# One core, banded attention and two MLPs: a planned order for all engines, and gate and value in seven block products out of eight

## The chip, the core and the metric

The kernel runs on one core of a Trainium2 chip. TensorE (PE in the profile) multiplies; its stationary operand is loaded by separate instructions (PEld). VectorE (DVE), ScalarE (ACT) and GpSimd (POOL) work on elements, and SyncE (SP) issues the transfers. Each engine runs its instructions in the order of the program and waits on semaphores for the others. The metric is device time in microseconds of one execution; less is better. The median of three runs of the kernel before is 694.55 us (694.54 to 695.88).

## What is computed

Sixteen attentions of 768 tokens (two batches, eight heads of 64), where a query sees itself and the 95 keys before it, and the first 8 keys of its sequence; then an MLP with a squared relu, a normalisation, and a gated MLP. All is float32 to the reference's accuracy.

```python
scores = scale * q @ k.T + bias;  scores = where(is_global | is_local, scores, -1e9)
a = softmax(scores);  x = (a @ v)                     # 1536 tokens x 512
h = maximum(x @ w_in, 0);        x = (h * h) @ w_out  # 512 -> 2048 -> 512
xn = x / sqrt(mean(x * x) + 1e-6) * rms_g
g = xn @ w_gate;  x = (g * sigmoid(g) * (xn @ w_val)) @ w_out2   # 512 -> 1536 -> 512
```

## The kernel before

Every product of the MLPs is taken in three: each operand is kept as a rounded high part and a low part (float32r), and `mm3` adds high by high, high by low and low by high (L158 to L160). A product has a stationary block of 128x128 and 512 moving columns. The tokens are handled in three chunks `c` of 512.

**Weights** come as float64 blocks of 128x512 (68 of them). `Weights.split` turns one into its two float32r parts: an absolute value on ACT (L103), four steps on DVE (L104 to L110), a rounding copy on ACT (L112) and a subtraction on DVE (L113). Eight slots, then sixteen, hold them.

**Attention** goes by 48 tiles of 128 queries and two heads. `qk` (L453) makes six score products of up to 256 columns, two heads side by side in the array; DVE adds the bias and takes the extreme (L458); ACT takes the exponential (L462); `scale` inverts the sums (L471, L472) and POOL multiplies by them (L474); `transpose` (L484) turns the blocks on TensorE and ACT copies them out (L486); `pv` (L499) multiplies by the values, and once a chunk and head pair is full, ACT and DVE split the result (L506, L507). POOL also rounds the keys and queries (L431) and builds the biases (L536, L541).

**The first MLP** (`stage1`) runs over 4 groups `g` of hidden blocks and the chunks: four hidden blocks (`ph`, 48 products), relu and square split into two parts, and four output blocks (`py`, 48 products) added to `y`. **The normalisation** (`queue_norm`) is a list of small steps that `tick` hands out between products; it has one product with a matrix of ones (`pn`, L276). **The second MLP** (`stage2`) runs over 4 groups and 3 chunks: for three blocks a gate product (`pg`) and a value product (`pv`, L160), Silu on ACT (L313), the multiplication on DVE (L320), the split, and the output product (`po`), added to `o` by DVE (L196).

**The order** is that of the program's text, which the tile framework's scheduler may then move. The text runs the attention as events; from event 60 on, each event gives the MLP a credit of 0.45 products of three (`RATE`, `MLP_FROM`). The 13 products of `warm_up` keep TensorE at work before the first scores.

Of the kernel before, what the change touches and what calls it, by code (L numbers as in the profile page):

```python
# [2 lines left out]

# [21 lines left out]
CH = 512  # L25
# [31 lines left out]
class Weights:  # L57
# [6 lines left out]
    LEAST = 2.0**-15  # L64
    MOST = float(np.array([0x47EFFFFF], np.int32).view(np.float32)[0])

    def __init__(self, nc, pool, srcs, slots):
        self.nc, self.pool, self.srcs = nc, pool, srcs
        self.stage, self.hl, self.slot = {}, {}, {}
        self.nload = self.nsplit = self.freed = 0  # L70
        self.idle = deque()
        self.nslots = 0
        self.add_slots(pool, slots)

    def add_slots(self, pool, slots):
        for _ in range(slots):
            self.idle.append((pool, self.nslots))
            self.nslots += 1

    def load(self):  # L80
        n = self.nload
        if n >= len(self.srcs):
            return
        t = self.pool.tile([P, 512, 2], I32, tag="wraw", bufs=2, name=f"wraw{n}")
        src = self.srcs[n].bitcast(I32)
        self.nc.sync.dma_start(out=t.rearrange("p c w -> p (c w)"), in_=src)
        self.stage[n] = t
        self.nload += 1

    def split(self):  # L90
        n = self.nsplit
        if n >= len(self.srcs) or not self.idle:
            return False
        while self.nload <= n:
            self.load()
        nc = self.nc
        raw = self.stage.pop(n)
        pool, s = self.slot[n] = self.idle.popleft()
        t = self.pool.tile([P, 512], I32, tag="wbits", bufs=2, name=f"wbits{n}")
        hi = pool.tile([P, 512], F32R, tag=f"whi{s}", bufs=1, name=f"whi{n}")  # L100
        lo = pool.tile([P, 512], F32R, tag=f"wlo{s}", bufs=1, name=f"wlo{n}")
        low, high = raw[:, :, 0], raw[:, :, 1]
        nc.scalar.activation(f32(t), f32(high), AF.Abs)  # L103
        nc.vector.tensor_scalar(  # L104
            out=f32(t), in0=f32(t), scalar1=self.LEAST, scalar2=self.MOST, op0=ALU.max, op1=ALU.min)
        nc.vector.tensor_scalar(
            out=t, in0=t, scalar1=3, scalar2=0x3FFFFFF8, op0=ALU.logical_shift_left, op1=ALU.bitwise_and)
        nc.vector.scalar_tensor_tensor(  # L108
            out=t, in0=low, scalar=29, in1=t, op0=ALU.logical_shift_right, op1=ALU.bitwise_or)
        nc.vector.scalar_tensor_tensor(  # L110
            out=t, in0=high, scalar=-(1 << 30), in1=t, op0=ALU.bitwise_and, op1=ALU.bitwise_or)
        nc.scalar.copy(hi, f32(t))  # L112
        nc.vector.tensor_tensor(out=lo, in0=f32(t), in1=f32(hi), op=ALU.subtract)  # L113
        self.hl[n] = (hi, lo)
        self.nsplit += 1
        self.load()
        return True

    def get(self, n):
        while self.nsplit <= n:  # L120
            assert self.split(), (n, self.freed)
        return self.hl[n]

    def free(self, n):
        for i in range(self.freed, n):
            self.hl.pop(i)
            self.idle.append(self.slot.pop(i))
        self.freed = max(self.freed, n)


class Mlp:
    def __init__(self, nc, main, late, psum, weights, gcol, epst, ones, out):
        self.nc, self.main, self.late, self.psum = nc, main, late, [psum]
        self.banks = {psum: MB}
        self.w, self.gcol, self.epst, self.ones, self.out = weights, gcol, epst, ones, out
        self.x = {}
        self.xk = {}
        self.z = {}
        self.y = {}
        self.bg = deque()  # L140
        self.zdone = set()
        self.tick_n = 0

    def new_act(self, c, name):
        hi = self.main.tile([P, KD, CH], F32R, tag="acth", bufs=NC_, name=f"{name}h{c}")
        lo = self.main.tile([P, KD, CH], F32R, tag="actl", bufs=NC_, name=f"{name}l{c}")
        return hi, lo
# [22 lines left out]
    def ready(self, c, k):  # L170
        return self.xk.get(c, 0) > k
# [693 lines left out]
```

## Time and profile before

| | us |
|---|---|
| median of three runs | 694.55 |
| the profiled execution, from the first to the last instruction (span) | 694.5 |
| TensorE busy | 676.2 (97%) |
| VectorE, ScalarE, GpSimd busy | 434.0, 298.3, 85.8 |
| last attention product ends, about | 164 |
| last product of all begins | 686.4 |

The profiled execution's time and its span agree with the median of the runs, so that sums are made against 694.5. An engine's busy time counts instructions in flight; products of TensorE overlap, and so 97% busy doesn't say that it works at its peak. What a product costs is read from the distance between the starts of two that follow each other. The granted clock is 1.00 for 2.4 GHz and 0.50 for 1.2 GHz.

### The profile page before, as it was taken

How to read it: one execution, taken by the hardware profiler on the slowest of the kernel's cores; microseconds unless marked ns; L12 is line 12 of the kernel's file. 1: busy time of each engine (PE TensorE's matmuls, PEld its weight loads, DVE VectorE, ACT ScalarE, POOL GpSimd, SP SyncE). 2: the span in 40 equal slices, each digit the busy share in tenths (PEclk: the TensorE clock that was granted, in tenths of full speed). 3: DMA queues.
4: the chain of work that ended last, by engine and by line, in shares of the span. 5: the costliest groups of instructions: out<-in, count | busy, mean ns of one | idle time of the engine just before them, and what ended most of it. 6: DMA issues, size and time to landing. Idle time of an engine off the chain costs nothing.

```text
span 694.5 us, 9041 instructions
## 1 busy us (share of the span) xinstructions
PE 676.2 (97%) x3283; PEld 538.4 (78%) x3283; DVE 434.0 (62%) x949; ACT 298.3 (43%) x625; POOL 85.8 (12%) x154
## 2 busy tenths in 40 slices
PE   6999999999999999999999999999999999999995
PEld 4666676676888888888888888888888888888884
DVE  6678936656889598448878995386239833322232
ACT  4555955866764254224456563443114411211110
POOL 6654724541000000000000000000000000000000
PEclk8568999999999999999999999999999999999998
DMA  7334523111334133004400221044003200001011
GB/s 245 125 129 158 187 72 105 60 63 56 128 121 135 49 100 112 30 1 122 121 1 20 73 91 61 4 147 122 0 1 114 98 1 0 1 1 60 1 60 67
DMA packets 16421, 52.84 MB, mean 76 GB/s; under 512 B 2416, under 2 KB 2928, under 8 KB 16368
## 3 DMA queue, kind: packets, MB, share of 16 engines
q1 hardware_dynamic: 16368, 52.18, 22.8%
q8 instruction: 28, 0.46, 0.3%
q14 instruction: 25, 0.20, 0.1%
HBM read 49.03 MB, written 3.15 MB: 75 GB/s over the span
## 4 chain that ended last, share of the span: by engine, by line
PE 75%; DVE 0%; ACT 0%; issue 0%; DVEq 0%
PE py L158 6%; PE py L160 6%; PE py L159 6%; PE ph L158 5%; PE ph L160 5%; PE ph L159 5%; PE pg L159 5%; PE pv L159 5%; PE pg L158 5%; PE pv L158 5%; PE pg L160 5%; PE pv L160 5%; PE po L158 5%; PE po L159 5%; PE po L160 5%; PE pn L276 0%
## 5 line engine op out<-in xcount | busy, mean ns | idle before, releaser
L159 PE MATMUL ph<-xl,whi 128*128 128x512 f32 x192 | 77.1, 402 | 0.0
L158 PE MATMUL ph<-xh,whi 128*128 128x512 f32 x192 | 75.5, 405 | 1.4 <-ACT xh L506 1.1
L160 PE MATMUL ph<-xh,wlo 128*128 128x512 f32 x192 | 75.6, 395 | 0.0
L103 ACT ACTIVATE wbits<-wraw 128x512 f32<-128x512 f32 x68 | 45.7, 673 | 69.5 <-DMA wraw<-in_w_out_dram 19.5
L320 DVE TENSOR_TENSOR s<-pv,sg 128x512 f32<-128x512 f32 x36 | 24.8, 689 | 70.3 <-PE pv L160 70.2
L112 ACT CAST whi<-wbits 128x512 fp32r<-128x512 f32 x68 | 41.9, 617 | 57.7 <-PE ph L159 22.8
L474 POOL TENSOR_SCALAR p<-p,rs 128x256 f32<-128x256 f32 (+1 forms) x96 | 55.9, 594 | 55.7 <-DVE rs L472 30.4
L113 DVE TENSOR_TENSOR wlo<-wbits,whi 128x512 fp32r<-128x512 f32 x68 | 46.4, 684 | 19.8 <-ACT whi L112 19.6
L462 ACT ACTIVATE p<-p,mn 128x256 f32<-128x256 f32 (+1 forms) x96 | 46.7, 488 | 23.8 <-DVE mn L458 22.6
L158 PE MATMUL pg<-zh,whi 128*128 128x512 f32 x144 | 56.4, 392 | 0.0
L160 PE MATMUL pg<-zh,wlo 128*128 128x512 f32 x144 | 56.0, 389 | 0.0
L159 PE MATMUL pg<-zl,whi 128*128 128x512 f32 x144 | 56.0, 389 | 0.0
L159 PE MATMUL pv<-zl,whi 128*128 128x512 f32 x144 | 56.0, 389 | 0.0
L160 PE MATMUL pv<-zh,wlo 128*128 128x512 f32 x144 | 56.0, 389 | 0.0
L158 PE MATMUL pv<-zh,whi 128*128 128x512 f32 x144 | 56.0, 389 | 0.0
L458 DVE CUSTOM_DVE_ANT_0 p<-ps,bw 128x256 f32<-128x256 f32 x80 | 32.5, 419 | 33.0 <-PE ps L453 27.6
L313 ACT ACTIVATE sg<-pg 128x512 f32<-128x512 f32 x36 | 21.5, 596 | 70.9 <-PE pg L160 70.6
L110 DVE SCALAR_TENSOR_TENSOR wbits<-wraw,wbits 128x512 int32<-128x512 int32 x68 | 47.2, 694 | 0.7
L108 DVE SCALAR_TENSOR_TENSOR wbits<-wraw,wbits 128x512 int32<-128x512 int32 x68 | 47.1, 693 | 0.2
L196 DVE TENSOR_TENSOR o<-po,o 128x512 f32<-128x512 f32 x36 | 22.7, 685 | 37.3 <-PE po L160 37.3
L158 PEld LDWEIGHTS ph<-xh,whi 128*128 128x128 f32 x192 | 36.2, 191 | 9.8 <-ACT xh L506 1.6
L159 PEld LDWEIGHTS ph<-xl,whi 128*128 128x128 f32 x192 | 36.4, 190 | 9.2 <-issue 2.1
(130 smaller groups left out, 1477.9 us busy)
## 6 DMA issues: line engine op xcount, KB each, us to landing
wraw<-in_w_out_dram SPq DMA_DIRECT2D x28, 512.0 KB, 3.4
wraw<-in_w_in_dram SPq DMA_DIRECT2D x16, 512.0 KB, 3.5
wraw<-in_w_gate_dram SPq DMA_DIRECT2D x12, 512.0 KB, 3.5
wraw<-in_w_val_dram SPq DMA_DIRECT2D x12, 512.0 KB, 3.5
v<-in_vab_dram SPq DMA_DIRECT2D x8, 512.0 KB, 3.6
out_dram<-o SPq DMA_DIRECT2D x12, 256.0 KB, 2.2
raw<-in_kq_dram SPq DMA_DIRECT2D x4, 624.0 KB, 3.8
raw<-in_kq_dram SPq DMA_DIRECT2D x4, 608.0 KB, 3.6
```

The source lines that it names most:

```text
L103: nc.scalar.activation(f32(t), f32(high), AF.Abs)
L108: nc.vector.scalar_tensor_tensor(out=t, in0=low, scalar=29, in1=t, op0=ALU.logical_shift_right, op1=ALU.bitwise_or)
L110: nc.vector.scalar_tensor_tensor(out=t, in0=high, scalar=-(1 << 30), in1=t, op0=ALU.bitwise_and, op1=ALU.bitwise_or)
L112: nc.scalar.copy(hi, f32(t))
L113: nc.vector.tensor_tensor(out=lo, in0=f32(t), in1=f32(hi), op=ALU.subtract)
L158: nc.tensor.matmul(ps, lhsT=w[0], rhs=a[0], start=first, stop=False)
L159: nc.tensor.matmul(ps, lhsT=w[0], rhs=a[1], start=False, stop=False)
L160: nc.tensor.matmul(ps, lhsT=w[1], rhs=a[0], start=False, stop=last)
L320: nc.vector.tensor_tensor(out=s, in0=pv, in1=sg, op=ALU.mult)
L458: nc.vector.tensor_tensor_reduce(out=p[:, j, :w], in0=ps[j][:, :w], in1=bias, scale=-0.125, scalar=3.0e38, op0=ALU.add, op1=ALU.min, accum ...
L462: nc.scalar.activation(p[:, j, :w], p[:, j, :w], AF.Exp, bias=mn[:, j : j + 1], scale=-1.0, accum_out=sm[:, j : j + 1])
L474: nc.gpsimd.tensor_scalar(out=p[:, j, :w], in0=p[:, j, :w], scalar1=rs[:, j : j + 1], scalar2=1.0, op0=ALU.mult, op1=ALU.mult)
```

## The change

1. **A plan sets the order on every engine.** All work is first recorded as operations (`Plan.add`) with an engine, an estimated duration, what they read and write, and a due time. `solve` runs a list scheduling over the estimates, and `emit` writes the operations in the order of their planned starts. The framework's own scheduler is off for this part (`manual_schedule`). Attention tiles have due times from `FIRST`, `PACE0` and `PACE1`.
2. **Chunks of 384 tokens**, four instead of three. The two products of the first MLP now have 384 moving columns. The output product of the second keeps 512.
3. **The first MLP begins earlier and is spread.** As soon as the attention of a chunk is complete, the 96 products of group 0 for that chunk stand between the attention steps of the next chunk (chunks 0 to 2).
4. **Gate and value by the Strassen-Winograd scheme.** Two weight blocks and two chunks form a 2x2 block product, done in seven products (`PRODUCTS`) instead of eight. Sums of weight blocks are made by POOL and split (`pair`), sums of activations likewise (`norm`); partial results are joined in PSUM by copies on ACT and additions on DVE (`quad`).
5. **Low parts on POOL.** Most of the subtractions that make the low part of a weight move from DVE to POOL, which has no such operation before.
6. **Squares on ACT.** `relu2` is three ACT operations and one on DVE for all groups.
7. **Fillers.** 76 products of a zeroed tile stand in gaps of the plan up to its 30th microsecond, in place of the 13 of `warm_up`.

```diff
-CH = 512
+CH = 384
+FIRST, STEP, PACE0, PACE1 = 8.0, 2.0, 2.1, 2.9
+FILL = 30.0
...
+class Plan:
...
+    def solve(self):
+        for o in reversed(self.ops):
+            for q in o.succ:
+                o.due = min(o.due, q.due - o.dur - (o.lat if q.eng != o.eng else 0.0))
...
+            t, e = best
+            while wait[e] and wait[e][0][0] <= t:
+                o = heappop(wait[e])[2]
+                heappush(ready[e], (o.due, o.n, o))
+            o = heappop(ready[e])[2]
...
+            if e == "PE" and t < FILL and filling:
+                x = max(free[e], 1.0)
+                while x + 0.2 < t:
+                    self.fill.append(x)
+                    x += 0.18
...
+    def emit(self, filler=None):
+        todo = [(o.start, 1, o.n, o.emit) for o in self.ops]
+        if filler:
+            todo += [(x, 0, i, filler) for i, x in enumerate(self.fill)]
+        for x in sorted(todo, key=lambda x: x[:3]):
+            x[3]()
...
+PRODUCTS = {
+    1: ("A11", "B11"), 2: ("A12", "B21"), 3: ("S4", "B22"), 4: ("A22", "T4"),
+    5: ("S1", "T1"), 6: ("S2", "T2"), 7: ("S3", "T3")}
...
+    def split(self, src, dst, n, rs, ws, eng):
+        e, t = (nc.vector, DVE) if eng == "DVE" else (nc.gpsimd, POOL2)
+        self.op("ACT", ACT(n), lambda: nc.scalar.copy(dst()[0], src()), rs, [(x, "hi") for x in ws])
+        self.op(eng, t(n), lambda: e.tensor_tensor(
+            out=dst()[1], in0=src(), in1=f32(dst()[0]), op=ALU.subtract), rs + [(x, "hi") for x in ws], [(x, "lo") for x in ws])
...
+    def pair(self, key, slots):
+        a, ra = self.expand()
...
+        self.split(a, sl.get, 512, ra, sl.res, "POOL")
+        keep(("A11", "A12"), sl)
+        b, rb = self.expand()
...
+        add(R(s, 0), R(b, 0), R(b, 1), ALU.add, rb, rs)
+        add(R(s, 1), R(s, 0), R(a, 0), ALU.subtract, rs + ra, rs)
+        sl2 = slots()
+        self.split(s, sl2.get, 512, rs, sl2.res, "POOL")
+        keep(("S1", "S2"), sl2)
+        sl3 = self.half_slot()
+        self.split(R(b, 1), lambda: tuple(two(t) for t in sl3.get()), 256, rb, sl3.res, "DVE")
+        keep(("A22",), sl3, 1)
+        add(R(b, 0), R(a, 0), R(b, 0), ALU.subtract, ra + rb, rb)
+        add(R(b, 1), R(a, 1), R(s, 1), ALU.subtract, ra + rs + rb, rb)
+        sl4 = slots()
+        self.split(b, sl4.get, 512, rb, sl4.res, "POOL")
+        keep(("S3", "S4"), sl4)
...
+    def quad(self, key, p, banks, sink):
+        self.product(1, b1, key, p, True)
+        self.op("ACT", ACT(CH), lambda: nc.scalar.copy(ps[b2](), ps[b1]()), rb(b1), rb(b2))
+        self.product(5, b3, key, p, True)
+        self.op("ACT", ACT(CH), lambda: nc.scalar.copy(p5(), ps[b3]()), rb(b3), r5)
+        self.product(6, b2, key, p, False)
+        self.op("DVE", DVE(CH), lambda: nc.vector.tensor_tensor(
+            out=ps[b3](), in0=ps[b2](), in1=p5(), op=ALU.add), rb(b2) + r5, rb(b3))
+        self.product(2, b1, key, p, False)
+        sink(0, 0, ps[b1], rb(b1))
+        self.product(7, b2, key, p, False)
+        self.op("DVE", DVE(CH), lambda: nc.vector.tensor_tensor(
+            out=t(), in0=ps[b2](), in1=p5(), op=ALU.add), rb(b2) + r5, rt)
+        sink(1, 1, t, rt)
+        self.product(3, b3, key, p, False)
+        sink(0, 1, ps[b3], rb(b3))
+        self.product(4, b2, key, p, False)
+        sink(1, 0, ps[b2], rb(b2))
...
+        plan.add("DVE", 0.5, lambda: nc.vector.memset(f32(tl(f"h{HB - 1}")), 0.0), (), [("h", HB - 1)])
...
+        plan.add("DVE", 0.7, count, (), ["nl"])
...
+        plan.solve()
```

A *round* below is one value of `fp` in the new second MLP: two weight blocks of gate and two of value, for both pairs of chunks (`p` 0 and 1), and their output products. There are six. Nine slots (`M0` to `M8`) hold the weights of a round, which fill eight of them, so that the next round's weights go into slots that the running round gives free.

How instructions stand in the program, at three places:

On DVE at the program's start, before: the zeroed tile of the warm-up (`warm`) stands first, ahead of the conversion of the two counts (`nf`, `nt`, `nv`).

```order
L602 MEMSET warm 128x512
L521 TENSOR_SCALAR mask_ra_102<-mask_hh_103 128x256
L522 TENSOR_TENSOR mask_ra_102<-mask_ra_102,mask_hh_103 128x256
L576 CAST nf<-nw 128x4
L580 TENSOR_SCALAR nt<-nf 128x2
```

On DVE at the start, now: `h_91` is the zeroed tile that the fillers read.

```order
L900 CAST nf<-nw 128x4
L902 TENSOR_SCALAR nt<-nf 128x2
L903 TENSOR_TENSOR nt<-nt,nf 128x2
L904 SCALAR_TENSOR_TENSOR nv<-nt,nf 128x2
L1066 MEMSET h_91 128x768
L858 TENSOR_SCALAR y_106<-y_87 128x256
```

The zeroed tile moved behind the four instructions on the counts, the first of which waits for a transfer.

On PE in the middle of the attention, before: `ps` are scores, `av` the product with the values, `pt` transposes.

```order
L453 MATMUL ps_0_1223<-kqh_1095 128x256
L453 MATMUL ps_0_1223<-kql_1096,kqh_1095 128x256
L453 MATMUL ps_0_1223<-kqh_1095,kql_1096 128x256
L453 MATMUL ps_1_1224<-kqh_1095 128x256
L453 MATMUL ps_1_1224<-kql_1096,kqh_1095 128x256
L453 MATMUL ps_1_1224<-kqh_1095,kql_1096 128x256
L499 MATMUL av_1156<-ptt_1210,v_893 64x128 x2
L484 MATMUL pt_1252<-ident,p_1188 128x128 x2
L453 MATMUL ps_0_1267<-kqh_1095 128x256
```

On PE at the like place now (`tb` are transposes, `b` are banks of the MLP's products, `xh` and `xl` the parts of the activations):

```order
L831 MATMUL av<-pt_248,v_147 64x128 x4
L315 MATMUL b_562<-xh_647,M_423 128x384
L316 MATMUL b_562<-xl_648,M_423 128x384
L317 MATMUL b_562<-xh_647,M_423 128x384
L822 MATMUL tb<-ident,p_200 128x128 x4
L315 MATMUL b_599<-xh_647,M_540 128x384
L316 MATMUL b_599<-xl_648,M_540 128x384
L317 MATMUL b_599<-xh_647,M_540 128x384
L795 MATMUL ps_162<-kqh_188 128x256
L795 MATMUL ps_164<-kqh_188 128x256
L795 MATMUL ps_162<-kql_222,kqh_188 128x256
```

Products of the MLP in threes or sixes now stand between all attention steps of a tile, and the six scores of a tile stand together.

On POOL at the end of the attention, before: the last row is the flag that ends the program.

```order
L474 TENSOR_SCALAR p_1957<-p_1957,rs_1990 128x256 x2
L474 TENSOR_SCALAR p_1995<-p_1995,rs_2032 128x256 x2
L790 TENSOR_LOAD flag
```

On POOL in the second MLP, now: sums of weight blocks (L387) and low parts (L306) of one pair of weights.

```order
L387 TENSOR_TENSOR wbits_417<-wbits_347 128x2x128
L387 TENSOR_TENSOR wbits_417<-wbits_417,wbits_531 128x2x128
L306 TENSOR_TENSOR M_661<-wbits_531,M_661 128x512
L387 TENSOR_TENSOR wbits_347<-wbits_531,wbits_347 128x2x128
L387 TENSOR_TENSOR wbits_347<-wbits_531,wbits_417 128x2x128
L306 TENSOR_TENSOR M_802<-wbits_347,M_802 128x512
L306 TENSOR_TENSOR M_735<-wbits_417,M_735 128x512
```

POOL had nothing to do after the attention; now each round has sixteen instructions there, eight of 512 columns and eight of 256.

## Rows read from the trace of the kernel before

**Rows 1.** Windows: us, busy time of each engine with its instructions, granted clock, DMA.

```profile
11.50:42.20 30.70, 27.75 (x113) 18.77 (x114) 21.13 (x70) 16.27 (x49) 18.35 (x29) 0.50 0.42 148
...
55.90:110.00 54.10, 52.14 (x356) 37.75 (x355) 37.77 (x124) 36.92 (x102) 27.16 (x43) 1.00 0.40 133
110.00:165.00 55.00, 54.15 (x419) 36.90 (x417) 31.78 (x137) 39.84 (x118) 25.73 (x48) 1.00 0.19 63
...
412.00:686.90 274.90, 274.82 (x1213) 227.24 (x1211) 127.36 (x213) 73.40 (x124) 0.00 (x0) 1.00 0.13 44
```

**Rows 2.** Windows of line L158 alone, after the attention: PE busy (count), PEld busy (count), clock.

```profile
164.20:694.50 530.30, 286.79 (x763) 143.23 (x763) 1.00 0.19 62
```

**Rows 3.** Timeline of PE in the second MLP: start, us, engine, line, operation.

```profile
599.62 0.39 PE L158 MATMUL pg<-zh,whi 128*128 128x512 f32 x1
...
601.43 0.39 PE L160 MATMUL pg<-zh,wlo 128*128 128x512 f32 x1
```

**Rows 4.** Timeline of one head's scores, with the loads of the stationary operand (PEld).

```profile
115.69 0.28 PE L453 MATMUL ps<-kql,kqh 64*128 64x256 f32 x1
115.70 0.19 PEld L453 LDWEIGHTS ps<-kqh,kql 64*128 64x128 f32 x1
115.81 0.27 PE L453 MATMUL ps<-kqh,kql 64*128 64x256 f32 x1
```

**Rows 5.** Timeline of PE between attention steps and products of the MLP.

```profile
116.02 0.96 PE L158 MATMUL ph<-xh,whi 128*128 128x512 f32 x3
116.91 0.38 PE L453 MATMUL ps<-kqh 64*128 64x256 f32 x1
...
117.46 0.66 PE L484 MATMUL pt<-ident,p 128*128 128x128 f32 x4
117.87 0.48 PE L159 MATMUL ph<-xl,whi 128*128 128x512 f32 x1
...
119.10 0.39 PE L160 MATMUL ph<-xh,wlo 128*128 128x512 f32 x1
119.42 0.66 PE L499 MATMUL av<-ptt,v 128*64 128x128 f32 x8
120.01 0.39 PE L453 MATMUL ps<-kqh 64*128 64x256 f32 x2
...
120.56 0.33 PE L484 MATMUL pt<-ident,p 128*128 128x128 f32 x1
```

**Rows 6.** Timeline of the start: DVE and PE; in brackets idle time and releaser.

```profile
1.46 4.76 PE L605 MATMUL warm_ps<-warm 128*128 128x512 f32 x13 [1.46 <-DVE warm L602]
...
3.68 0.17 DVE L576 CAST nf<-nw 128x4 f32<-128x4 int32 x1 [1.63 <-DMA nw<-in_counts_dram]
...
6.34 0.33 PE L453 MATMUL ps<-kqh 64*128 64x128 f32 x2
```

**Rows 7.** Timeline of the end: last product of PE, last four transfers.

```profile
686.43 0.39 PE L160 MATMUL po<-whi,sp_2l 128*128 128x512 f32 x1
686.57 2.38 SPq L344 DMA_DIRECT2D out_dram<-o  x4
```

**Rows 8.** Groups by line and shape: busy us, mean ns of one, idle before and releaser.

```profile
L474 POOL TENSOR_SCALAR p<-p,rs 128x256 f32<-128x256 f32 x80 | 48.8, 622 | 46.8 <-DVE rs L472 25.1 <-ACT p L462 8.9 <-PE av L499 4.1
...
L104 DVE TENSOR_SCALAR wbits<-wbits 128x512 f32<-128x512 f32 x68 | 29.0, 427 | 20.0 <-ACT wbits L103 19.5
...
L320 DVE TENSOR_TENSOR s<-pv,sg 128x512 f32<-128x512 f32 x36 | 24.8, 689 | 70.3 <-PE pv L160 70.2
...
L284 DVE RECIPROCAL rin<-rms 128x512 f32<-128x512 f32 x3 | 10.0, 3349 | 1.7 <-ACT rms L279 1.7
...
L431 POOL TENSOR_SCALAR kqh<-raw 128x512 fp32r<-128x512 f32 x12 | 8.2, 687 | 3.5 <-DMA raw<-in_kq_dram 3.5
```

**Rows 9.** The same groups of line L108 on DVE, up to 165 us and after it.

```profile
L108 DVE SCALAR_TENSOR_TENSOR wbits<-wraw,wbits 128x512 int32<-128x512 int32 x10 | 7.4, 743 | 0.0
L108 DVE SCALAR_TENSOR_TENSOR wbits<-wraw,wbits 128x512 int32<-128x512 int32 x58 | 39.7, 684 | 0.2
```

More of the change, by code (lines that the diff above doesn't have):

```diff
@@ new lines, with __init__, define, __call__ @@
+LAT = {"PE": 0.27, "DVE": 0.17, "ACT": 0.22, "POOL": 0.22, "SP": 2.2, "END": 0.0}
+DVE = lambda n: 0.07 + n / 960
+FAST = lambda n: 0.12 + n / 1920
+ACT = lambda n: 0.10 + n / 1200
+POOL1 = lambda n: 0.15 + n / 800
+POOL2 = lambda n: 0.10 + n / 370
+DMA = lambda kb: 0.3 + kb / 200.0
+class Lazy:
+    def __init__(self):
+        self.made, self.how = {}, {}
+    def define(self, name, pool, shape, dtype):
+        self.how[name] = (pool, shape, dtype)
+    def __call__(self, name):
+        if name not in self.made:
+            pool, shape, dtype = self.how[name]
+            self.made[name] = pool().tile(shape, dtype, tag=name, bufs=1, name=name)
+        return self.made[name]
@@ L439, in at, with bias, tile @@
         return s, t, c, hp, PLANS[c][0][t]
-    def qk(self, n):
-        nc, pool = self.nc, self.pool
+    def bias(self, h, i):
+        nc, tl = self.nc, self.tl
+        name, src, w = (f"bw{h}", "rel", W) if i else (f"bo{h}", "t0", P)
+        if name not in self.plan.wrote:
+            self.op("POOL", POOL1(w), lambda: nc.gpsimd.tensor_scalar(
+                out=tl(name), in0=tl(src), scalar1=-slope8(h), scalar2=1.0, op0=ALU.mult, op1=ALU.mult), [src], [name])
+        return name
+    def tile(self, n, due):
+        nc, tl = self.nc, self.tl
@@ new lines, in build @@
+    def build(self):
+        n = len(self.slices)
+        due = lambda i: FIRST + PACE0 * i if i < HP * NT else FIRST + PACE0 * HP * NT + PACE1 * (i - HP * NT)
+        self.load(0)
+        self.load_v(0)
+        self.load(1)
+        self.prep(0)
+        self.masks()
+        for s in range(n):
+            for t in range(NT):
+                self.tile(s * NT + t, due(s * NT + t))
+                if t == 0 and s + 1 < n:
+                    self.prep(s + 1)
+                    self.load_v(s + 1)
+                    if s + 2 < n:
+                        self.load(s + 2)
+            yield s
@@ new lines @@
+        att = Attention(nc, plan, tl, ap, psa, mlp, kq, vab, ident, nl, ng)
+        plan.add("DVE", 0.5, lambda: nc.vector.memset(f32(tl(f"h{HB - 1}")), 0.0), (), [("h", HB - 1)])
+        plan.add("POOL", 1.5, lambda: (make_identity(nc, ident), nc.gpsimd.memset(ones, 1.0), nc.gpsimd.memset(epst, 1.0e-6)),
+                 (), ["tb"], due=9.0)
+        plan.add("DVE", 0.7, count, (), ["nl"])
+        chunks = att.build()
+        for c in range(NC_):
+            for _ in range(HP):
+                next(chunks)
+            if c == 0:
+                plan.add("SP", 0.3, lambda: nc.sync.dma_start(out=gcol, in_=rms_g.rearrange("(e p) -> p e", p=P)), (), ["g"], due=40.0)
+            if c < NC_ - 1:
+                mlp.begin(c, [ends[c] + (ends[1] - ends[0]) / 32 * i for i in range(32)])
@@ L789 @@
+        end = plan.add("END", 0.0, ax.close, (), ["late"])
+        for o in att.mine:
+            end.deps.add(o)
+            o.succ.append(end)
+        mlp.rest(ends[NC_ - 1])
+        plan.solve()
+        h = lambda: tl(f"h{HB - 1}")
+        plan.emit(lambda: nc.tensor.matmul(
+            tl("b3")[:, :CH], lhsT=h()[:, :P], rhs=h()[:, :CH], start=True, stop=True, skip_group_check=True))
     flag = covered(nc, const, nl, ng)
```

1098 lines of the change are left out of this document (602 added, 496 removed).

## The prediction

> **What bounds the kernel now.** I read the windows first: the clock and TensorE's share by stage. After the attention TensorE never stands still, POOL does nothing, and VectorE is half busy [rows 1]. Then the spacing of products: two starts eight products apart lie 1.81 us apart, 0.2263 us each [rows 3], of which 512 columns at 2.4 GHz are 0.2133, so that 0.013 is fixed. After 164.2 us there are 3 x 763 = 2289 products [rows 2]: 518.0 us. From there to the end of the last product at 686.66 [rows 7] are 522.4, so that 4.4 go to the three normalisation products and the one wait at the start. That stage is TensorE's alone; it gets shorter by fewer columns and by nothing else.
>
> The attention is the other stage: 164 us, with 2448 - 2289 = 159 products of the MLP in it (36 us). Its TensorE looks full [rows 1], but what fills it is changes of kind. Six scores take 0.55 us until something else begins; a product with the values 0.59; four transposes 0.41 when a product of the MLP follows (0.585 when scores or values follow, the 0.17 more being a drain that the MLP has instead); three products of the MLP before scores 0.89, that is 0.21 above 3 x 0.2263; before the values the last one alone shows 0.32, 0.10 above [rows 5]. By such prices the 151 groups between 55.9 and 164.2 come to 102.7 us of 107.3 that they took. So at full clock the stage is work and drains, and 4.5% waits. At half clock, 30.7 us long [rows 1], the groups from 13.7 to 42.2, which these prices put at 15.7 us, took 27.4, a factor of 1.75.
>
> **The products after the change.** One of 384 columns streams for 0.160 us; with the fixed part 0.173. Below 0.160 it cannot be; above it could be the load of the stationary operand, which reads 0.19 us in every row, longer than 0.160. But scores of 256 columns with a load each start 0.12 apart [rows 4], so the next load runs beside and takes at most 0.12. I take 0.173.
> - First MLP: 1536 products at 0.173 = 265.7, before 1152 at 0.2263 = 260.7: 5 lost to fixed parts.
> - Gate and value: 12 weight pairs x 2 pairs of chunks x 7 x 2 x 3 = 1008 at 0.173 = 174.4, before 864 at 0.2263 = 195.5: 21 won.
> - Output: 432 of 512 as before, 97.8.
> Together 537.9 against 554.0: **16 us** is all that the arithmetic gives.
>
> **The attention after the change.** I took every group of TensorE's new order up to the last product with values and put the prices on it. Scores: 48 x 0.55 = 26.4. Transposes: 47 groups, 23 of them before the MLP or a filler, 22.2 (tiles at a sequence's start have half). Values: 26.3. The MLP's 288 products of chunks 0 to 2: 49.8, and 65 changes of kind after them, 47 at 0.21 and 18 (before transposes) at 0.10, 11.7. Fillers: 76 x 0.173 + 2.9 = 16.0. Sum **152.4 us**. So 50 us of MLP lie in it instead of 36, but it pays for each being put alone between two steps.
>
> It also starts later. The fillers read a tile that DVE now clears behind four instructions on the counts; the first of these waits for its transfer until 3.68 [rows 6]. Four of 0.17 to 0.2 end at 4.4, the clearing of 768 columns takes 0.5 to 1.0 (an operation of 512 columns reads 0.69 [rows 8]); I take 0.75: first filler at **5.2**, before 1.46. The slow clock of the first products cost 4.76 - 12 x 0.2263 - 0.39 = 1.65 before [rows 6]; **1.6** again. Thirty fillers stand ahead of the first scores, which so begin near 12.2 instead of 6.34.
>
> Waits: between a tile's scores and its transposes the order leaves 5 us or more of TensorE's work for nearly all tiles, and the chain through DVE, ACT, DVE and POOL needs about 4.4 (from scores to two multiplications of 0.62 on POOL [rows 8]). In the first chunk POOL has 27 us of biases, keys and multiplications for about 28. I take the 4.5% from above, **7 us**, between 3 and 14. The last product with values then ends at 5.2 + 1.6 + 152.4 + 7 = 166.2; before, 164. The first three blocks of chunk 3 wait for nothing, the fourth for the split of the last values: 0.7.
>
> **From there to the end.** 2256 products at 0.173 and 432 at 0.2263 are 488.1; the normalisations' products, four of three quarters the width instead of three, at most the 4.4 above, 2.6: **490.7**. Stalls:
> - In the first MLP four activations go through three ACT operations and one on DVE, about 2.4 us at three quarters of 0.6 to 0.69 [rows 8], and six groups of three products (3.1 us) lie between. Hidden; 1 us for all.
> - The second normalisation stands between the MLPs. The sum, the root with its table, three reciprocals (3/4 of 3.35 [rows 8]), two products with the weights, a split: 9.8 us to the first part of chunk pair 1; the order has 10.5 us of other products ahead of it. Its second half needs seven POOL operations more, 18.2 against 17.5. **2 us**, 0 to 6.
> - POOL's two-operand operations don't occur in the trace. Below they cannot be cheaper than one operand of 512, 0.69 [rows 8]; above, twice the one-operand row of 256 columns for each operand, 4 x 0.622 = 2.5 [rows 8]. I take two operands at the 512-column row, 1.37, which has the width in question, and 0.91 for 256 columns. Eight of each are 18.2 us of POOL in a round of 45.4 us of TensorE (168 x 0.173 + 72 x 0.2263). The next round's gate sums need a slot that is free after seven products of the second pair of chunks, 7.3 us; then POOL has 4.6 us for the rest of gate and 7.6 for value: 19.5. TensorE asks for the value weights at 22.7 + 4.2 = 26.9. So nothing need wait; but operations of 2.0 us and more would be too late. I put one late POOL instruction, 1.2, on each of five changes of round: **6 us**, 0 to 25.
>
> [...]
>
> The end: 7.8 us from the last product to the end before. Four additions and four transfers came at once (2.38 us of issue [rows 7]); now a tile is finished every 1.36 us and one is left: **7.1**, 6.6 to 7.8.
>
> **Sum:** 5.2 + 1.6 + 152.4 + 7 + 0.7 + 490.7 + 1 + 2 + 6 + 7.1 = **673.7 us**, 3% under the span, which agrees with the median of 694.55.
>
> **Rivals.**
> *Few waits.* The order keeps margins; with 3 us of waits in the attention and none at the rounds or the normalisation it is 673.7 - 4 - 9 = 661. For it: no wait at all in the stage before [rows 1].
> *VectorE becomes the bound of a round (slower).* Its work there: 24 conversion steps of 0.69 and 0.43, 13.5; 16 additions and multiplications and 8 subtractions of 384 columns, 12.7; 2 halves, 0.8; 12 additions to the output, 8.2: 35.2 of 45.4 [rows 8]. POOL works beside it for 18.2 us, where today it is idle. Beside POOL a step of DVE read 0.743 instead of 0.684 [rows 9], 0.06 with POOL half busy at 0.62 each; with operations twice as long 0.15 on 34 steps, 5 us: 40 of 45.4, not the bound. If each of POOL's operations held up DVE for its whole length, 53.4: 8 us in five rounds, 708. From about 50 us a round the change is slower than before. [...]
> *The clock.* If the fillers don't hold 2.4 GHz through the first chunk, its 25 us take 1.75 times as long: + 18.5, 692, level with before. Against it: four fillers per tile there, more products than in the stretches that kept 1.00 [rows 1].
> *Loads bound.* If a product waits for its load, 0.192 instead of 0.173 on 2544 products: 722; slower from 0.181. Against it [rows 4].
>
> **How the numbers follow.** Forecast 673.7, own range 664 to 684: 0.50. Few waits (655 to 664): 0.19. Sums of the terms' far ends, 684 to 693: 0.09. Clock (688 to 698): 0.08. VectorE (695 to 715): 0.11. Loads: 0.03. The range 656 to 700 leaves out some 0.05 below and 0.12 above. A measurement of this kernel tells 0.2% (1.4 us) from no change: faster 0.82, same 0.04, slower 0.14.
>
> **What would show it.** First filler at 5.2 and first scores at 12; clock 1.00 from 9 us on; last product with values at 160 to 172; products of 384 columns 0.173 apart; POOL's 512-column subtraction at 1.1 to 1.8; a round of 45 to 47 us. Wrong if a round takes over 50, if TensorE waits over 15 us in the attention, or if the spacing is above 0.18.

## The result and the profile after

The changed kernel takes 701.23 us (median of four runs, 700.51 to 702.33), the kernel before 695.21 beside it: a ratio of 1.0072, 95% interval 1.0047 to 1.0097. It is **slower by 0.7%**, where 673.7 us was forecast with 656 to 700 around it. The profiled execution has a span of 698.9 us.

The page's busy times, the stages by windows (us, then busy time and instructions of PE, PEld, DVE, ACT and POOL, the granted clock, DMA), and the timeline's ends (the first filler, the first scores, the last product, the last transfers):

```profile
PE 657.8 (94%) x3876; PEld 591.8 (85%) x3876; DVE 495.2 (71%) x1025; ACT 374.4 (54%) x834; POOL 248.5 (36%) x298
```

```profile
164.00:300.00 136.00, 133.85 (x769) 133.21 (x770) 77.30 (x135) 68.71 (x133) 11.72 (x9) 1.00 0.20 66
300.00:396.00 96.00, 88.52 (x495) 85.30 (x494) 79.91 (x114) 60.34 (x120) 47.19 (x40) 1.00 0.17 55
396.00:450.00 54.00, 45.23 (x223) 39.75 (x222) 48.37 (x67) 34.63 (x67) 35.55 (x30) 0.97 0.12 40
450.00:693.00 243.00, 236.51 (x1214) 215.37 (x1213) 172.23 (x290) 95.58 (x190) 69.54 (x66) 1.00 0.19 64
```

```profile
5.47 6.88 PE L1085 MATMUL b<-h 128*128 128x384 f32 x30 [5.47 <-DVE h L1066]
12.28 0.33 PE L795 MATMUL ps<-kqh 64*128 64x128 f32 x2
...
692.40 0.39 PE L317 MATMUL b<-M,h 128*128 128x512 f32 x1
...
692.19 1.78 SPq L592 DMA_DIRECT2D out_dram<-y  x2
```

The kernel before had 274.82 us of TensorE in 274.90 in the like stage [rows 1]. Now TensorE stands still in every stage behind the attention, most of all between 300 and 450 us. VectorE is busy for 71% of the span, and for 83% and 90% of the two windows from 300 to 450 us; its busy time includes the time that an instruction of it is held up (1.62 us instead of 0.55 in the rows below). Two starts of products lie 0.1733 us apart at 384 columns (median), as forecast. At 512 columns the closest stretches of eight products have 0.2266; the median of single distances is 0.230, a little more than the forecast 0.2263. What goes beyond 0.1733 and 0.2266 by more than 0.02 us, summed over the products behind the last one with the values (which starts at 162.44 us) to the end, is **36.7 us**; 9.7 were forecast. I call this sum *the stalls* below, and give it for every run. About 2 us of it are in every run the own time of the normalisation's products.

Whom TensorE waits for there, in the view of waits (us in total, times, longest):

```profile
PE b L316 <- DVE h L415: 5.4, 6, 1.6
PE b L466 <- DVE ns L464: 5.4, 3, 2.2
PE b L315 <- DVE ra L542: 5.2, 9, 1.0
PE b L317 <- DVE h L306: 3.9, 2, 3.3
PE b L315 <- DVE y L588: 3.0, 4, 0.7
```

All five are links that VectorE makes. Why they come late is seen where one of them does. The timeline in the first MLP, with VectorE's and GpSimd's rows under TensorE's:

```profile
206.64 0.34 PE L315 MATMUL b<-h,ar 128*128 128x384 f32 x1
208.56 0.44 PE L316 MATMUL b<-h,ar 128*128 128x384 f32 x1 [1.58 <-DVE h L415]
...
204.89 0.55 DVE L415 TENSOR_TENSOR h<-ra,h 128x384 fp32r<-128x384 f32 x1
...
206.88 1.62 DVE L415 TENSOR_TENSOR h<-ra,h 128x384 fp32r<-128x384 f32 x1
...
206.73 1.36 POOL L306 TENSOR_TENSOR M<-wbits,M 128x512 fp32r<-128x512 f32 x1 [4.82 <-ACT M L305]
```

The same subtraction takes 0.55 us at 204.89 and 1.62 at 206.88. GpSimd began the low part of a weight 0.15 us before the second one and ended it at 208.09; VectorE's, 1.07 us longer than the other, ended 0.41 us after that. And in each round, 47.87 us apart (591.12, 638.98 and so on):

```profile
591.12 1.72 DVE L349 SCALAR_TENSOR_TENSOR wbits<-wraw,wbits 128x512 int32<-128x512 int32 x1
592.87 0.69 DVE L352 SCALAR_TENSOR_TENSOR wbits<-wraw,wbits 128x512 int32<-128x512 int32 x1
593.48 1.28 DVE L588 TENSOR_TENSOR y<-b,y 128x512 f32<-128x512 f32 x2
...
591.00 1.29 POOL L306 TENSOR_TENSOR M<-wbits,M 128x512 fp32r<-128x512 f32 x1 [5.61 <-ACT M L305]
...
594.22 0.50 PE L315 MATMUL b<-M,h 128*128 128x512 f32 x1 [0.74 <-DVE y L588]
```

Here a step that nobody needs soon (a weight of the next round) is held for 1.03 us, and the addition that frees a bank of TensorE's stands two places behind it.

Which operations this befalls is read from the views of single lines (minimum, median and maximum in ns, first and last start):

```profile
L415 DVE TENSOR_TENSOR h<-ra,h x52: 524/558/1631, 167.9 to 389.6; 128x384 fp32r<-128x384 f32 x52
L349 DVE SCALAR_TENSOR_TENSOR wbits<-wraw,wbits x57: 679/693/1739, 166.5 to 639.0; 128x512 int32<-128x512 int32 x57
L345 DVE TENSOR_SCALAR wbits<-wbits x57: 410/427/1510, 165.6 to 634.8; 128x512 f32<-128x512 f32 x57
L588 DVE TENSOR_TENSOR y<-b,y x60: 677/691/692, 477.5 to 692.8; 128x512 f32<-128x512 f32 x60
L472 DVE RECIPROCAL ns<-ns x12: 894/918/953, 346.4 to 408.1; 128x128 f32<-128x128 f32 x12
```

Of the 52 at line 415, nine start while GpSimd works. One of them meets only the last 0.11 us of a GpSimd operation and takes 0.52 us; the eight others take 1.09 to 1.63, and the 43 outside stay at or under 0.56. Of the 60 at line 588, with one operand in PSUM (`b`), fifteen start beside GpSimd and none takes over 0.692. Of the twelve reciprocals at line 472, whose one operand is in SBUF, four start beside it, and the longest takes 0.953, as it does without GpSimd (e1). The medians show nothing; the hold is in the maxima.

### The profile page after: what moved, and what is told of

Read it like the earlier page. It is cut to its first block, busy times and chain, and to the rows that moved or that the text cites. A ratio compares the mean times of both kernels' runs of the same rounds, so it can differ in the third digit from the quotient of the medians.

```text
span 698.9 us, 10714 instructions
## 1 busy us (share of the span) xinstructions
PE 657.8 (94%) x3876; PEld 591.8 (85%) x3876; DVE 495.2 (71%) x1025; ACT 374.4 (54%) x834; POOL 248.5 (36%) x298
## 4 chain that ended last, share of the span: by engine, by line
PE 31%; DVE 16%; ACT 2%; issue 2%; POOL 2%; POOLq 0%; DVEq 0%
PE b L315 10%; PE b L317 10%; PE b L316 10%; DVE wbits L349 3%; DVE h L306 2%; DVE ra L564 1%; DVE wbits L345 1%; DVE wbits L347 1%; DVE ns L472 1%; DVE xl L306 1%; DVE h L415 1%; DVE wbits L352 1%; DVE y L588 1%; DVE nq L493 1%; POOL nq L498 1%
## 5 line engine op out<-in xcount | busy, mean ns | idle before, releaser
L306 POOL TENSOR_TENSOR M<-wbits,M 128x512 fp32r<-128x512 f32 x60 | 82.0, 1371 | 254.3 <-ACT M L305 168.9
L315 PE MATMUL b<-xh,M 128*128 128x384 f32 x384 | 133.4, 347 | 1.2 <-DVE xl L306 1.2
L316 PE MATMUL b<-xl,M 128*128 128x384 f32 x384 | 129.1, 336 | 0.5 <-DVE xl L306 0.5
L317 PE MATMUL b<-xh,M 128*128 128x384 f32 x384 | 129.0, 336 | 0.0
L315 PEld LDWEIGHTS b<-xh,M 128*128 128x128 f32 x384 | 72.2, 188 | 6.9 <-issue 1.9
L316 PEld LDWEIGHTS b<-xl,M 128*128 128x128 f32 x384 | 72.4, 189 | 2.7 <-DVE xl L306 1.0
L415 DVE TENSOR_TENSOR h<-ra,h 128x384 fp32r<-128x384 f32 x64 | 42.3, 666 | 42.9 <-ACT ra L414 42.7
L317 PEld LDWEIGHTS b<-xh,M 128*128 128x128 f32 x384 | 72.4, 188 | 0.1
L305 ACT CAST M<-wbits 128x512 fp32r<-128x512 f32 x68 | 41.9, 617 | 49.5 <-DVE wbits L352 27.1
L588 DVE TENSOR_TENSOR y<-b,y 128x512 f32<-128x512 f32 x60 | 40.9, 688 | 28.2 <-PE b L317 27.9
L317 PE MATMUL b<-M,h 128*128 128x512 f32 x144 | 56.9, 395 | 3.9 <-DVE h L306 3.9
L315 PE MATMUL b<-M,h 128*128 128x512 f32 x144 | 56.9, 395 | 3.1 <-DVE y L588 3.0
L316 PE MATMUL b<-M,h 128*128 128x512 f32 x144 | 56.8, 394 | 0.0
L344 ACT ACTIVATE wbits<-wraw 128x512 f32<-128x512 f32 x68 | 45.4, 668 | 18.1 <-DMA wraw<-in_w_gate_dram 7.5
L316 PE MATMUL b<-h,ar 128*128 128x384 f32 x128 | 43.5, 339 | 3.4 <-DVE h L415 3.4
```

The lines of the kernel that those rows point to most:

```text
L305: self.op("ACT", ACT(n), lambda: nc.scalar.copy(dst()[0], src()), rs, [(x, "hi") for x in ws])
L306: self.op(eng, t(n), lambda: e.tensor_tensor(out=dst()[1], in0=src(), in1=f32(dst()[0]), op=ALU.subtract), rs + [(x, "hi") for x in ws], [ ...
L315: nc.tensor.matmul(ps, lhsT=wh, rhs=ah, start=first, stop=False, skip_group_check=True)
L316: nc.tensor.matmul(ps, lhsT=wh, rhs=al, start=False, stop=False, skip_group_check=True)
L317: nc.tensor.matmul(ps, lhsT=wl, rhs=ah, start=False, stop=last, skip_group_check=True)
L415: self.op("DVE", DVE(CH), lambda: nc.vector.tensor_tensor(out=get()[1], in0=t(), in1=f32(get()[0]), op=ALU.subtract), rt + hi, lo)
```

## Experiments

*Lock* is the theory: GpSimd's operations hold those of VectorE that have no operand in PSUM (the reciprocals aside), and so VectorE's links come too late in an order that was planned without this. Its rivals: *Margins* (the order leaves the links too little time, whatever GpSimd does) and *Late GpSimd* (GpSimd's own results come late).

| run | median us | ratio to before (95%) | stalls us |
|---|---|---|---|
| the change | 701.23 | 1.0072 (1.0047 to 1.0097) | 36.7 |
| e1: all two-operand work on VectorE | 675.60 | 0.9686 (0.9626 to 0.9746) | 10.8 |
| e2: low parts alone on VectorE | 682.82 | 0.9784 (0.9725 to 0.9842) | 17.5 |
| e3: GpSimd only fills | 671.09 | 0.9625 (0.9565 to 0.9685) | 6.1 |
| e4: the fill first | 700.69 | 1.0035 (1.0001 to 1.0068) | 39.8 |
| e5: e1 + idle two-operand work | 703.51 | 1.0094 (1.0076 to 1.0112) | 40.8 |
| e6: e1 + idle one-operand work | 685.42 | 0.9834 (0.9816 to 0.9852) | 21.8 |
| e7: e1 + e4 | 673.22 | 0.9668 (0.9648 to 0.9687) | 10.4 |
| e8: one operand of line 415 in PSUM | 691.77 | 0.9928 (0.9911 to 0.9945) | 26.4 |
| e9: e7, eight products | 690.60 | 0.9908 (0.9877 to 0.9939) | 2.9 |
| e10: the plan knows the hold | 688.20 | 0.9884 (0.9854 to 0.9913) | 21.9 |
| e11: the change, eight products | 703.65 | 1.0110 (1.0081 to 1.0139) | 13.2 |

The kernel before had medians of 695.21 to 696.98 us in the four groups of runs, so that differences of under 2 us between runs of two groups say little. The groups are: the change; e1 to e4; e5 to e8; e9 to e11. TensorE's mean granted clock was 0.995 to 0.997 in the runs of the change and lower in several others (0.983 to 0.989 in e10, 0.983 to 0.987 in e5), so that a part of some differences is clock.

### e1 and e2: take the work off GpSimd

```diff
-                self.block((kind, g * G1 + f), slot, "DVE" if g < 2 else "POOL")
+                self.block((kind, g * G1 + f), slot, "DVE")
...
-        self.split(a, sl.get, 512, ra, sl.res, "POOL")
+        self.split(a, sl.get, 512, ra, sl.res, "DVE")
...
-        add = lambda o, x, y, op, r, w: self.op("POOL", POOL2(256), lambda: nc.gpsimd.tensor_tensor(
+        add = lambda o, x, y, op, r, w: self.op("DVE", DVE(256), lambda: nc.vector.tensor_tensor(
```

(and so for the other splits and for `diff`; e2 leaves `add`, the last two lines here, and `diff` on GpSimd.)

> Every two-operand operation that GpSimd has behind the attention (64 subtractions of 512 columns, 32 of 384, 48 sums of 256) goes to VectorE; the order is planned anew with that. Theory Lock (a GpSimd operation with two operands in SBUF keeps VectorE's operations with operands in SBUF waiting until it ends, so VectorE's links come late in a fixed order): VectorE's subtractions at line 415 all take 0.55 us and its line 349 0.69, the stalls of TensorE behind the attention fall from 38 us to 5 to 12, although VectorE has 64 x 0.61 + 48 x 0.34 + 32 x 0.47 = 70 us more to do; 668 to 676 us. Rival Margins (the order leaves VectorE's links too little time, whatever GpSimd does): 70 us more work on the engine that is late makes more stalls, 701 to 720 us.

> Only the low parts (64 of 512 columns, 16 of 384) go from GpSimd to VectorE; the 48 sums and 16 differences stay, 55 us of GpSimd's 161 us with two operands. Lock: the stalls fall with that time, from 38 us to 13 to 18; 677 to 685 us. Margins: 46 us more on VectorE, 701 to 712 us.

Both came in at Lock's numbers: 675.60 and 682.82 us, stalls 10.8 and 17.5. In e1 VectorE has 70 us more to do, and its lines read

```profile
L415 DVE TENSOR_TENSOR h<-ra,h x52: 492/558/562, 169.0 to 377.4; 128x384 fp32r<-128x384 f32 x52
L349 DVE SCALAR_TENSOR_TENSOR wbits<-wraw,wbits x57: 680/692/694, 167.6 to 616.4; 128x512 int32<-128x512 int32 x57
```

The maximum of line 349 is 694 instead of 1739. The page's busy times say what the holds were worth to VectorE:

```profile
PE 653.1 (97%) x3876; PEld 594.6 (88%) x3876; DVE 508.2 (75%) x1169; ACT 372.1 (55%) x832; POOL 84.5 (13%) x154
```

With 70 us more work (the estimate above; operations of VectorE that follow each other start 0.60 to 0.61 us apart at 512 columns in the change, 0.47 at 384 and 0.33 to 0.34 at 256) it is busy only 13 us longer (495.2 in the change), so that 57 us of its busy time were waiting. Added up over VectorE's operations in the trace of the change, what goes beyond the undisturbed length of each is 55 us, which agrees. A full VectorE isn't the cause either. Between 300 and 396 us e1 has it busy for 89.56 us of 96, where the change had 79.91, and TensorE for 95.86:

```profile
300.00:396.00 96.00, 95.86 (x543) 93.74 (x543) 89.56 (x171) 68.56 (x135) 0.00 (x0) 1.00 0.19 61
```

So Margins is out as the main cause. Late GpSimd isn't out: these results no longer come from GpSimd.

### e3: GpSimd writes without reading

```diff
+        if eng == "POOL":
+            go = lambda: e.memset(f32(dst()[1]), 0.0)
```

(and so for `add` and `diff`.)

> The order of the changed kernel as it is, but each of GpSimd's subtractions and sums behind the attention only writes a constant (a fill with no operand): the low parts of the weights and of half of the normalised values, and the sums of weights and values, are left out. Lock: no operation of VectorE is drawn out, its busy time falls by about 45 us, stalls 38 to 8 to 14 us, 674 to 680 us. Margins: VectorE's own links are as before, stalls over 30 us, 696 to 702 us.

671.09 us, stalls 6.1: 3 us better than Lock's range. I had set the fills too dear. They take 0.53 us, and line 417 (415 in the change) is never held:

```profile
L417 DVE TENSOR_TENSOR h<-ra,h x52: 493/559/568, 168.3 to 378.1; 128x384 fp32r<-128x384 f32 x52
L348 DVE TENSOR_SCALAR wbits<-wbits x57: 416/422/775, 166.0 to 605.2; 128x512 f32<-128x512 f32 x57
L307 POOL MEMSET M<- x60: 520/526/767, 166.7 to 616.6; 128x512 f32 x60
```

One form, the one-operand step of the weights at line 348, is still held at times, up to 775 ns for a median of 422. The order of the changed kernel is untouched here on TensorE, VectorE and ScalarE, so that 30 of its 36.7 us of stalls go with GpSimd's reads and the length of its operations; this run doesn't part the two, and GpSimd's own results come earlier too.

### e5 and e6: put the suspect back, with results that nobody reads

```diff
+        if extra:
+            scr = lambda: self.tl("scr")[:, :n]
+            self.op("POOL", POOL2(n), lambda: nc.gpsimd.tensor_tensor(
+                out=scr(), in0=f32(dst()[0]), in1=f32(dst()[0]), op=ALU.subtract),
+                [(x, "hi") for x in ws], ["scr"])
```

> The kernel of e1 (all of it on VectorE, 675.6 us), and beside it GpSimd subtracts the high part of each weight block (64 of 512 columns) and of 12 normalised values (384 columns) from itself into a scratch tile that nobody reads: about 64 x 1.3 + 12 x 1.3 = 99 us of two-operand work whose results no engine waits for. Lock: VectorE's operations with operands in SBUF are drawn out again to up to 1.4 us beside it, and the stalls come back by 99/161 of what e1 took away or more, since VectorE now also has the work itself: 690 to 712 us. Rival Late GpSimd (the changed kernel lost its time because GpSimd's own results came late and their readers waited): nothing reads these results, 674 to 677 us.

> As e5, but the idle work has one operand (a multiplication by one of the same tile, the form of lines 764 and 815). The theory Lock says two operands in SBUF; if one operand holds the path too, VectorE's operations are drawn out by this as well and the time is 680 to 700 us; if only two do, 674 to 678 us. In the attention the one-operand form took up to 1.39 us beside VectorE's work instead of 0.48, so I expect some: 678 to 690 us.

703.51 us: **idle work on GpSimd costs 28 us**, and the stalls are back at 40.8. (The run has 16 normalised values in it, not 12; GpSimd's busy time is 103.9 us above e1's.) So late results aren't needed to lose this time. In the change they aren't what TensorE waits for either: its view of waits names no operation of GpSimd. Late GpSimd is out as the main cause. Lines of e5, then of e6:

```profile
L421 DVE TENSOR_TENSOR h<-ra,h x52: 495/558/1395, 168.9 to 391.4; 128x384 fp32r<-128x384 f32 x52
L311 POOL TENSOR_TENSOR scr<-M x60: 1042/1369/1718, 192.4 to 653.1; 128x512 f32<-128x512 f32 x60
```

```profile
L421 DVE TENSOR_TENSOR h<-ra,h x52: 495/558/965, 169.5 to 382.9; 128x384 fp32r<-128x384 f32 x52
L311 POOL TENSOR_SCALAR scr<-M x60: 621/990/1287, 192.9 to 634.5; 128x512 f32<-128x512 f32 x60
L594 DVE TENSOR_TENSOR y<-b,y x60: 672/686/693, 470.9 to 679.4; 128x512 f32<-128x512 f32 x60
```

One operand on GpSimd holds too, for the shorter time that it takes (median 0.990 us instead of 1.369; line 421 at most 0.965 instead of 1.395): 685.42 us. So "two operands on GpSimd" was too narrow; in these runs a read of one operand in SBUF was enough on that side, and the longer operation held for longer.

### e8: one operand in PSUM

```diff
+        sq, rq = (src, rsrc) if self.attention_over else (t, rt)
-        self.op("ACT", ACT(CH), lambda: nc.scalar.activation(t(), t(), AF.Square), rt, rt)
+        self.op("ACT", ACT(CH), lambda: nc.scalar.activation(sq(), t(), AF.Square), rt, rq)
```

> The changed kernel, GpSimd's work as it is; only the full-precision square of the first MLP's activation is written back to its PSUM bank behind the attention, so that the subtraction at line 415 has one operand in PSUM. Lock (only operations with all operands in SBUF wait for GpSimd, as the 60 at line 588 with one in PSUM that never took over 0.70 us suggest): line 415 takes 0.55 us throughout, the 6.4 us of stalls that wait for it go, 694 to 697 us. Rival (VectorE as a whole is slowed or too full): line 415 keeps its 1.3 to 1.6 us cases, 700 to 702 us.

691.77 us, stalls 26.4. With GpSimd's work as it was, the line is free (thirteen of its operations start beside GpSimd), and its neighbours are held as before:

```profile
L416 DVE TENSOR_TENSOR h<-b,h x52: 494/557/558, 168.4 to 384.9; 128x384 fp32r<-128x384 f32 x52
L349 DVE SCALAR_TENSOR_TENSOR wbits<-wraw,wbits x57: 681/693/1741, 167.1 to 629.3; 128x512 int32<-128x512 int32 x57
```

The gain is 2 us more than expected. TensorE's waits for this line fell from 5.4 to 1.9 us and didn't vanish. The plan also came out with another order here: its stalls over 0.25 us between the MLPs fell from 9.4 to 3.9 us, and those of the rounds rose from 8.1 to 10.5. Which part of the gain is the operand's alone isn't separated.

### e10: leave the work, tell the plan

```diff
+            if o.lock:
+                t = max(t, held)
+                held = t + o.dur
             o.start = t
```

> The changed kernel with all work on the engines where it was; only the planner knows that an operation with its operands in SBUF on VectorE and a two-operand operation on GpSimd exclude each other (each starts behind the other in the plan). Lock: the order then has VectorE's links where they come in time, and the stalls of the rounds and of the first MLP shrink, while those around the normalisation, where both engines are full, stay: 38 to 14 to 25 us, 680 to 690 us. Rival (the wait is in the work itself; no order helps): over 697 us.

688.20 us, as Lock has it. Line 420 (415 in the change) is still held, 1658 ns at the most, but TensorE now waits 0.7 us for it instead of 5.4. What stays lies mostly between the MLPs, in the first three rows:

```profile
PE b L320 <- DVE ra L569: 5.0, 1, 5.0
PE b L321 <- DVE xl L310: 2.8, 1, 2.8
PE b L320 <- ACT xh L309: 1.9, 2, 1.6
...
PE b L321 <- DVE h L420: 0.7, 1, 0.7
```

The page's busy times:

```profile
PE 655.9 (96%) x3876; PEld 595.0 (87%) x3876; DVE 484.1 (71%) x1025; ACT 378.1 (55%) x836; POOL 246.8 (36%) x298
```

VectorE's busy time falls by 11 us against the change, so that the new order avoids some holds and leaves most of them. With the same work and most of the holds, a plan that knows of them gets 13 us back; taking the work away gets 26. About half of the loss was thus for the order to avoid.

### e9 and e11: eight products instead of seven

Gate and value as plain sums over `k`, without sums of weights or values (`quad` loops over four `k` for each block and chunk), on e7 and on the changed kernel.

> e7 with the gate and value products done as eight block products (no sums of weights or values, no copies of partial products): 6 rounds x 2 x 2 x 6 = 144 more products of 384 columns at 0.173 us = 24.9 us, less the part of e7's 10 us of stalls that the scheme's own steps cause (the chain of the second normalisation at 393 to 399 us, 4 to 6 us). If the seven products are worth their arithmetic once VectorE is not held up: 673.2 + 24.9 - 5 = 693, 690 to 696 us. Rival (their extra steps cost most of what they win): under 685 us.

> The changed kernel with gate and value as eight block products, the weights' low parts on GpSimd as it has them: 52 two-operand operations of 512 columns (71 us) in place of 161 us. 24.9 us more of products; by Lock the stalls fall with GpSimd's time, from 38 to 10 to 17 us: 701 + 25 - (21 to 28) = 698 to 705, so that the seven products win next to nothing in the changed kernel. Rival (the scheme's arithmetic arrives, the stalls come from the new order alone): 720 to 726 us.

Both as expected. Undisturbed, the seven products are worth 690.60 - 673.22 = 17 us: 24.9 of arithmetic less 7.5 of stalls that go without them. In the changed kernel they are worth 703.65 - 701.23 = 2 us, little more than the kernel before differs between these two groups: with them GpSimd works 164.0 us behind the attention (11.72 + 47.19 + 35.55 + 69.54 in the windows above), in e11 only 69.2 on its low parts, and the stalls (36.7 against 13.2) ate the rest.

### e4 and e7: the start

```diff
-        plan.add("DVE", 0.5, lambda: nc.vector.memset(f32(tl(f"h{HB - 1}")), 0.0), (), [("h", HB - 1)])
+        plan.add("DVE", 0.5, lambda: nc.vector.memset(f32(tl(f"h{HB - 1}")), 0.0), (), [("h", HB - 1)],
+                 due=-10.0)
```

> VectorE's fill of the tile that the warming products read stands ahead of the conversion of the counts, as in the kernel before. The first warming product, now at 5.5 us because the fill waits for the counts' load, comes at 1.5 to 2 us, TensorE's clock is up sooner, and the first scores (12.3 us) come where their operands are there. If these are set by warming: 2 to 3 us less, 698 to 699 us. If they are set by the load of the first keys and the mask (rival): scores at 12 us as now, 701 us. Both theories of the stalls leave them at 38 us.

> e1 and e4 together: everything with two operands on VectorE, and the fill ahead of the counts' conversion. With stalls of 11 us only, TensorE's clock should stay up behind the attention, so the 2.5 us that e4 won there are not given back: 672 to 673.5 us. Rival: the clock falls again at the one stall that is left at 397 to 402 us and for longer, 675 us.

e4 missed: 700.69 us instead of 698 to 699. The start did what it should:

```profile
1.72 8.14 PE L1086 MATMUL b<-h 128*128 128x384 f32 x30 [1.72 <-DVE h L1066]
9.79 0.33 PE L795 MATMUL ps<-kqh 64*128 64x128 f32 x2
```

and the last product with values starts 2.5 us earlier, at 159.92. The profiled execution lost this again in two places, with the same order of products in both kernels. About 1.4 us went behind the wait for the first normalisation's product, where the granted clock was 0.50 from 340 to 342 us, against 1.00 in the change (0.99 in the mean from 300 to 415 us, against 1.00). About 1.6 went behind a stall of 3.5 us that both kernels have near 417 us, where it got the lower clock for longer (windows of e4, then of the change):

```profile
415.00:427.00 12.00, 8.18 (x28) 6.89 (x27) 10.38 (x13) 5.16 (x11) 8.73 (x9) 0.73 0.00 0
```

```profile
415.00:427.00 12.00, 8.22 (x36) 6.95 (x35) 10.38 (x15) 5.45 (x12) 8.75 (x8) 0.86 0.00 0
```

Where the mean granted clock of a run is the same, the gain is there: at 0.995 e4's runs took 698.24 and 698.89 us, those of the change 701.78 and 702.33; at 0.997 one of 697.28 stands against 700.51 and 700.68. Six of e4's ten runs had 0.991 or less, none of the change's. So the start is worth about 3 us at the same clock; why it falls for longer in some executions wasn't settled. In e7, on top of e1, it gave 2.4 us and came in as expected (the times of the two don't overlap, but they are of different groups, and the intervals of their ratios do overlap): **673.22 us, 3.3% under the kernel before**. This is the best complete kernel of the study.

## Why the prediction was wrong

**Right.** First filler 5.47 (5.2), first scores 12.28 (12.2), clock 1.00 but for 0.97 in one window. The last product with values starts at 162.44; 166.2 was forecast for its end, so that this stage took 3 us less. The spacings are 0.1733 and 0.230 (0.173 and 0.2263). GpSimd's subtraction of 512 columns takes 1.37 us in the mean, the very value that was taken. That is partly luck: undisturbed it takes about 1.29 us (1.280 to 1.302 in 38 of the change's 64 low parts), and VectorE's holding it in its turn (1.336 to 1.605 in the other 26) makes up the mean. Its group of line 306:

```profile
L306 POOL TENSOR_TENSOR M<-wbits,M 128x512 fp32r<-128x512 f32 x60 | 82.0, 1371 | 254.3 <-ACT M L305 168.9 <-DVE h L415 74.5 <-PE b L317 6.0
```

From the end of the last product's columns, 692.40 + 0.23, to the end are 6.3 us (7.1). Every part of the arithmetic arrived; e1 shows it at 675.6.

**The step that failed** is the one on stalls, 1 + 2 + 6 + 0.7 = 9.7 us, which measured 36.7. Of the forecast, 0.7 was for the wait behind the last values, which the sum leaves out (1.2 us in the trace), and the own time of the normalisation's products, about 2 us of the 36.7, had its own 2.6; like for like it is about 35 against 9. The stalls over 0.25 us make 31.7 of them: 6.7 in the first MLP's activations (forecast 1), 7.5 at the normalisation's products (no wait forecast; 5.9 of them are waits), 9.4 between the MLPs and in the first round (2), 8.1 in the later rounds (6). That the last number is near its forecast is luck: the 6 were put down to GpSimd's own lateness, and in the later rounds TensorE waits for VectorE alone. What no term of the sum had is that GpSimd's new work holds VectorE's operations, 55 us in all.

None of the prediction's three signs of being wrong came. A round took 47.87 us (over 50 was the sign), TensorE stood still for about 5 of the 144 us of the attention from 20 to 164 us (over 15), and the spacing was 0.1733 (above 0.18). The time went where no sign had been set, in the first MLP, at the normalisation and between the MLPs.

**Where in the working.** The rival on VectorE had the right mechanism, and was weighed down by three readings.
- *The price was a mean.* "0.743 instead of 0.684" [rows 9] was read as 0.06 a step. Seven of those ten read 0.67 to 0.69, one 1.085:

```profile
L108 DVE SCALAR_TENSOR_TENSOR wbits<-wraw,wbits x10: 674/683/1085, 17.7 to 80.5; 128x512 int32<-128x512 int32 x10
```

The hold was rare and long: that one, which starts inside a GpSimd operation (line 431, 17.43 to 18.20 us), took 0.40 us more than the median. The trace of before had held steps in it, and their lengths were the ones to take.
- *It asked whether VectorE would be full.* "40 of 45.4, not the bound", and slower only "from about 50 us a round". A round takes 47.87 us, VectorE is at 172 of 243 us there, and time is lost all the same: in a fixed order a link that is 1.1 us late is paid at once if TensorE's next product is behind it (line 415 at 206.88 us, 1.07 longer, and TensorE waits 1.58 us for it). The threshold was one of throughput; the damage is one of lateness.
- *It priced the rounds alone.* Of the 31.7 us, 23.6 lie ahead of the later rounds, beside the low parts of groups 2 and 3, of the first weights of the second MLP, and beside the differences of the normalised values. The first MLP's stall term ("Hidden; 1 us for all") was worked out with VectorE's undisturbed 0.6 to 0.69.

What the trace shows beside this rival: one of the two engines was held until the other's operation ends (line 415's subtraction at 206.88 us ended 0.41 us behind GpSimd's operation and took 1.62 instead of 0.55), and operations with one operand in PSUM went free (line 588 at most 0.692 us, line 416 in e8 at most 0.558). One operand instead of two on VectorE didn't free it: line 345, whose operand is in SBUF, was held up to 1.51 us instead of 0.427. The rival's 708 us, for holds of the whole length of each GpSimd operation, was nearest to the 701, and its range, 695 to 715 with a chance of 0.11, holds it, though its price was put in the rounds.

## What to carry to other kernels

Before elementwise work goes from VectorE to an idle GpSimd, ask of each VectorE operation beside it whether it has an operand in PSUM; the others may each wait until the GpSimd operation ends (here up to 1.63 us instead of 0.55 at line 415, and 1.74 instead of 0.69 at line 349), and in a fixed order TensorE can pay for that without any engine being full (36.7 us of stalls with VectorE busy for 71% of the span). (Of the operations without one that start beside GpSimd behind the attention, only the reciprocals went free here.) Look at the maxima of a line rather than its mean, since a hold was rare and long here (eight of the 52 at line 415, with 1.09 to 1.63 us). If the work must stay, give the plan the exclusion as a rule (13 us here), or route the urgent operation through PSUM (9 us, a part of them from the new order); moving it back was worth 26.

## What the runs showed of the hardware

- Beside GpSimd, subtractions and additions with both operands in SBUF were held up to 1.64 us instead of 0.55 at 384 columns (line 306; 1.63 at line 415); reciprocals (maximum 0.953, four beside GpSimd) and operations with one operand in PSUM (maximum 0.692 at 512 columns) weren't.
- A GpSimd operation with one operand in SBUF held the subtraction too (e6: 0.965 for 0.558); a fill, which reads nothing, held the one-operand step of the weights at line 348 (e3: 0.775 for 0.422), not the subtraction (0.568 at most).
- GpSimd is held in its turn: of its 64 low parts of 512 columns in the change, 26 take 1.336 to 1.605 us, and all 26 start inside a VectorE operation of a kind that is held; the other 38 take 1.280 to 1.302.
- Products of 384 columns of float32r start every 0.1733 us, with a load of 128 columns for each; a load shows 0.19 us itself, longer than that distance, and so runs beside products.
- From 384 to 512 columns the distance grows by 0.0533 us (0.1733 to 0.2266), 2.40 columns a ns at a granted clock of 1.00. At 0.50, near 423 us of the change, products of 384 columns start 0.32 us apart, 1.20 columns a ns. The 2.4 and 1.2 GHz named with the granted clock are these rates of columns.
